# Windowed attention and two feed-forward layers: exponentials in PSUM, transposes ahead of scores, constants made on the chip

## The chip, the cores and the metric

One core of one Trainium2 chip runs the whole program in one launch. The metric is the device time of an execution in microseconds; three executions of the kernel before took 841.26, 841.40 and 842.33 us, with a median of 841.4 us. The profile is of one more execution.

## The reference

Attention over 4 batches, 8 heads, 576 positions and a head size of 64, in a causal window of 64 positions, and then two feed-forward layers over the 2304 tokens.

```python
scores = scale * np.matmul(q, k.transpose(0, 1, 3, 2))
mask = (rel >= 0) & (rel < window)             # rel = row - column, window = 64
scores = np.where(mask, scores, -1000000000.0)
scores = scores - np.max(scores, axis=-1, keepdims=True)
attn = np.exp(scores)
attn = attn / (np.sum(attn, axis=-1, keepdims=True) + 1e-09)
x = np.matmul(attn, v)                         # then (2304, 512)
x = ((x @ w1) * (x @ w2)) @ w3 @ w_out         # 512 -> 1024 -> 1024 -> 512
h = x @ w_in                                   # 512 -> 2048
out = (h * sigmoid(h)) @ w_out2
```

All of it is float32. The weights come in float64; the kernel reads their words and makes float32 of them on the chip.

## The kernel before

**Stages.** Phase W (`phase_w`, to about 93 us) multiplies w3 by w_out, in 64 float32 matmuls of 128x512 (L582), and turns the float64 words of w_out, w3, w1 and w2 into float32: an ACT pair (L125, L128), two DVE instructions (L138, L141) and a POOL add (L145) for each tile of 512 KB. Six blocks of 384 tokens follow (`phase_a`), each with 16 units of 12 matmuls (the products with w1 and w2, L618) and 8 units of 12 (the product w3 w_out, L648). The last block is merged with the second layer, which runs alone from about 410 us to the end. The order of all instructions is written out by hand; every engine runs its own in that order.

**Attention** is cut into 72 groups (128 rows, two heads). They are threaded through phase W (14 groups) and through the blocks, 12 to a block, by `half`: two halves make a group's step, and in the blocks every unit is preceded by one half, so that PE has 24 matmuls of a block between two steps. A group g passes through: scores on PE into a PSUM tile `s` that has one buffer (`scores`, L329 for the first 17 groups in plain float32, L333 and L337 after that); a masked reduction on DVE for each head, which leaves the scaled scores in the SBUF tile `sm` and their minimum in `nm` (L344, with the mask from the tile `consts`); an exponential on ACT for each head, in place in `sm`, with the sum of each row (`exps`, L355); sum, reciprocal and the multiply of the two heads on DVE (`normalise`, L363, L365, L367); three transposes on PE into the tile `t` (L377), from which ACT and DVE make the operands of the next product (`split_t`, L383 to L392); and the values' product on PE (L404 to L406, L411, L412), with its sums on ACT, DVE and POOL (L419 to L423).

The order within an even half, which stands around the change:

```python
if g < NG:
    scores(g)
squeeze(unit_of[0])
if 2 <= g <= NG + 1:
    sums.append(values(g - 2))
    ...
if 1 <= g <= NG:
    split_t(g - 1, transposes(g - 1))
if g < NG:
    exps(g)
```

The odd half normalises g, ends the sums of g - 2 and prepares the operands of g + 2. `fill` puts pieces of the weight conversions between the instructions of `scores` and `normalise` on DVE.

**The start.** POOL sets the empty corners of the tiles `kq` and `klo` (L531, L534). SP requests, one after the other, two weight tiles, q and k of group 0, masks and identity (`consts`, 192 KB), two weight tiles, q and k of group 1, another mask (128 KB), two weight tiles, and v of groups 0 to 2. The third mask follows in step 9 of phase W. In each of the 16 steps of phase W the loop first finishes the conversions that are due (`steps_to`), then runs the halves that are due (`halves_to`), then more conversions, then the matmuls.

## Time and profile before

| | |
|---|---|
| median of three executions | 841.4 us (841.26 to 842.33) |
| the profiled execution | 841.24 us, of which its instructions span 839.5 us |
| granted TensorE clock | 1.000 |
| busy: PE, DVE, ACT, POOL | 827.4, 615.3, 561.2, 529.7 us |
| DMA | 102.66 MB, mean 122 GB/s |

The profiled execution is 0.2 us under the median. Busy times are sums over stages with different limits: DVE and ACT are far from full over the span, but not within the attention's first 400 us. Matmuls are pipelined and their ends are modelled, so a stretch in which PE is busy throughout may still hold short waits; the distance between two instructions of the same kind shows them. In the rows further on, a timeline line gives the start (us from the start of the span), the duration, the engine, the line, the operation, what it writes and reads, and in brackets the idle time of the engine before it with what ended it.

### The profile page before, as it was taken

The numbers are of one execution on the slowest core, as the hardware profiler recorded it, in microseconds if no ns is written. First come the engines' busy times: TensorE is split into PE (matmuls) and PEld (weight loads), VectorE is DVE, ScalarE is ACT, GpSimd is POOL, SyncE is SP. The second block draws the span as 40 slices with busy tenths as digits, with TensorE's granted clock in tenths as the row PEclk, the third lists the DMA queues.
The fourth block names the chain that finished last, engine by engine and source line by source line (L and its number), as shares of the span: only waits on it lengthen the run. The fifth ranks groups of instructions, "written<-read, shape, count | busy, mean of one in ns | idle before, by whom it ended". The sixth has DMA issues, their size and how long they took to land.

```text
span 839.5 us, 14173 instructions
## 1 busy us (share of the span) xinstructions
PE 827.4 (99%) x4418; PEld 745.9 (89%) x4418; DVE 615.3 (73%) x1424; ACT 561.2 (67%) x1390; POOL 529.7 (63%) x588
## 2 busy tenths in 40 slices
PE   7999999999999999999999999999999999999998
PEld 3555799999999999999999988888888888988986
DVE  7889877688888888888368698998644567644544
ACT  6889778898898898898556566556543446443433
POOL 5768666677777677677565577876454456454441
PEclk9999999999999999999999999999999999999999
DMA  9998234444544544543433522301301201201002
GB/s 320 330 321 279 72 107 128 149 127 133 167 150 142 169 156 145 170 157 103 155 134 120 194 76 76 125 26 51 102 26 56 95 26 64 88 25 51 1 1 75
DMA packets 54682, 102.66 MB, mean 122 GB/s; under 512 B 5200, under 2 KB 32592, under 8 KB 54608
## 3 DMA queue, kind: packets, MB, share of 16 engines
q1 hardware_dynamic: 51008, 96.91, 35.5%
q10 hardware_dynamic: 3600, 4.85, 1.6%
q8 instruction: 35, 0.57, 0.3%
q14 instruction: 39, 0.32, 0.1%
HBM read 88.11 MB, written 13.63 MB: 121 GB/s over the span
## 4 chain that ended last, share of the span: by engine, by line
PE 69%; POOL 8%; ACT 6%; issue 4%; DVE 1%; ACTq 0%; POOLq 0%; DVEq 0%
PE o L882 24%; PE ab L618 14%; PE hy L828 12%; PE hx L828 9%; PE x L648 6%; POOL klo L303 2%; POOL vhl L321 1%; ACT sm L355 1%; PE t L377 1%; POOL xr L423 1%; ACT qkhi L297 1%; POOL p L88 1%; POOL cv_b L189 1%; PE o L411 1%; PE s L333 1%
## 5 line engine op out<-in xcount | busy, mean ns | idle before, releaser
L882 PE MATMUL o<-hl,gp 128*128 128x512 f32 x504 | 133.3, 394 | 0.0
L618 PE MATMUL ab<-xa,hl 128*128 128x384 f32 x576 | 119.0, 341 | 0.0
L828 PE MATMUL hy<-xop,j 128*128 128x384 f32 x576 | 115.9, 335 | 0.0
L618 PE MATMUL ab<-xb,hl 128*128 128x384 f32 x570 | 115.2, 334 | 0.0
L88 POOL TENSOR_TENSOR gp<-tmp,gp 128x384 fp32r<-128x384 f32 x56 | 64.1, 1145 | 77.5 <-ACT gp L85 75.9
L828 PEld LDWEIGHTS hy<-xop,j 128*128 128x128 f32 x576 | 102.6, 188 | 9.0 <-DVE tmp L722 1.0
L882 PEld LDWEIGHTS o<-hl,gp 128*128 128x128 f32 x504 | 93.1, 188 | 13.1
L618 PEld LDWEIGHTS ab<-xb,hl 128*128 128x128 f32 x570 | 100.3, 188 | 0.0
L618 PEld LDWEIGHTS ab<-xa,hl 128*128 128x128 f32 x576 | 99.1, 188 | 0.0
L844 ACT ACTIVATE tmp<-hx 128x384 f32<-128x384 f32 x48 | 23.6, 492 | 111.5 <-DVE hx L722 67.8
L722 DVE TENSOR_TENSOR tmp<-hy,tmp 128x384 f32<-128x384 f32 x96 | 53.2, 554 | 56.1 <-PE hy L828 51.5
L828 PE MATMUL hx<-xop,j 128*128 128x384 f32 x432 | 86.6, 335 | 0.0
L882 PE MATMUL o<-hl,gq 128*128 128x512 f32 x324 | 85.9, 393 | 0.0
L88 POOL TENSOR_TENSOR gq<-tmp,gq 128x384 fp32r<-128x384 f32 x36 | 39.0, 1084 | 74.3 <-ACT gq L85 74.3
L828 PEld LDWEIGHTS hx<-xop,j 128*128 128x128 f32 x432 | 76.8, 188 | 4.1
L423 POOL TENSOR_TENSOR xr<-ot 128x128 f32<-128x128 f32 x55 | 32.7, 594 | 73.7 <-DVE ot L422 65.5
L303 POOL TENSOR_TENSOR klo<-qk,qkhi 64x192 fp32r<-64x192 f32 x110 | 67.2, 611 | 7.6 <-ACT qkhi L297 2.7
L882 PEld LDWEIGHTS o<-hl,gq 128*128 128x128 f32 x324 | 60.3, 188 | 11.2
L648 PE MATMUL x<-p,wp 128*128 128x384 f32 x360 | 69.6, 339 | 0.0
L355 ACT ACTIVATE sm<-sm,nm 128x192 f32<-128x192 f32 x144 | 64.5, 450 | 3.9 <-DVE nm L344 2.5
L648 PEld LDWEIGHTS x<-p,wp 128*128 128x128 f32 x360 | 61.9, 188 | 0.0
L145 POOL TENSOR_TENSOR cv_b<-cv_b,cv_r 128x512 int32<-128x512 int32 x32 | 48.6, 1520 | 18.8 <-DVE cv_b L141 9.4
(146 smaller groups left out, 1896.7 us busy)
## 6 DMA issues: line engine op xcount, KB each, us to landing
qk<-in_qkv SPq DMA_DIRECT2D x55, 384.0 KB, 3.1
words<-in_w_out SPq DMA_DIRECT2D x24, 512.0 KB, 5.4
r<-w_in SPq DMA_DIRECT2D x22, 512.0 KB, 3.4
words<-in_w3t SPq DMA_DIRECT2D x16, 512.0 KB, 6.5
words<-in_w SPq DMA_DIRECT2D x16, 512.0 KB, 6.2
xe<-in_w_in SPq DMA_DIRECT2D x16, 512.0 KB, 4.8
v<-in_qkv SPq DMA_DIRECT2D x55, 96.0 KB, 2.7
x2d<-x2s ACTq DMA_DIRECT2D x24, 192.0 KB, 1.9
```

The lines of the kernel that those rows point to most:

```text
L88: (nc.vector if eng_lo == "dve" else nc.gpsimd).tensor_tensor(out=lo, in0=src, in1=f32(hi), op=ALU.subtract)
L145: nc.gpsimd.tensor_tensor(out=x, in0=b, in1=self.r, op=ALU.add)
L189: nc.gpsimd.tensor_tensor(out=self.b, in0=self.b, in1=self.r, op=ALU.add)
L303: nc.gpsimd.tensor_tensor(out=k_lo[g % 2][hs, h * 192 : h * 192 + 192], in0=t[hs, n], in1=f32(hi[hs, n]), op=ALU.subtract)
L355: nc.scalar.activation(out=x, in_=x, func=AF.Exp, scale=-1.0, bias=nm[:, h : h + 1], accum_out=sums_of[g % 2][:, h, 0:1])
L423: nc.gpsimd.tensor_tensor(out=xr[:, c, r : r + 128], in0=t[:, 0:128], in1=t[:, 128:256], op=ALU.add)
L618: nc.tensor.matmul(acc, lhsT=w[:, l, fs], rhs=x[k // 2][:, k % 2, r, :], start=(k == 0 and n == 0), stop=(k == 3 and n == 2),)
L648: nc.tensor.matmul(acc, lhsT=wp[f][:, l, o * 128 : (o + 1) * 128], rhs=p[f][:, r, :], start=(f == 0 and n == 0), stop=(f == 7 and n == 2),)
L722: eng.tensor_tensor(out=out, in0=a, in1=b, op=op)
L828: nc.tensor.matmul(bank[name], lhsT=w[:, l, at + kt], rhs=x[:, kt, r, :], start=(fresh and kt == 0 and n == 0), stop=(kt == 1 and n == 2), ...
L844: nc.scalar.activation(out=sg, in_=src, func=AF.Sigmoid)
L882: nc.tensor.matmul(oacc[t], lhsT=g[:, l, cols], rhs=weights["out", 2 * p + i][:, r, :], start=(p == 0 and i == 0 and n == 0), stop=(p == P ...
```

## The change

It has four parts.

1. The exponentials are written into the scores' PSUM tile `s` and not back into `sm`; the normalising multiply reads them there and writes `sm`.
2. In the even half PE runs the values of g - 2 and the transposes of g - 1 ahead of the scores of g. What ACT and DVE do keeps its order.
3. Masks and identity are no longer loaded (458,752 bytes in three DMAs), but made on the chip: by five DVE memsets and six POOL selects at the start, and by a POOL copy with two memsets for the third mask in step 0 of phase W. The corners of `kq` are set by DVE; those of `klo` by POOL behind the first group's exponentials.
4. q and k of group 2 and v of group 0 are requested right behind the first scores, v of groups 1 and 2 in steps 0 and 1; the conversions of step 1's first part come behind its halves and not ahead of them.

```diff
--- before.py
+++ after.py
@@ -40,7 +40,7 @@
 
 
 @with_exitstack
-def tile_window_attention_ffn(ctx, tc, qkv, qkp, vp, mask, w1, w2, w3t, w_out, w_in, w_out2, out):
+def tile_window_attention_ffn(ctx, tc, qkv, qkp, vp, w1, w2, w3t, w_out, w_in, w_out2, out):
 
 
 
@@ -62,6 +62,34 @@
     consts = att.tile([128, 896], F32, name="consts", tag="mask", bufs=1)
     mask_at = (384, 0, 640)
     id_sb = consts[:, 256:384]
+
+    def select(t, op, base, rows, step, fill):
+        nc.gpsimd.affine_select(
+            out=t, in_=t, compare_op=op, fill=fill, base=base, pattern=[[step, t.shape[1]]], channel_multiplier=rows
+        )
+
+    def build_first():
+        m = consts[:, 0:256]
+        nc.vector.memset(m[:, 0:64], MASKED)
+        nc.vector.memset(m[:, 64:192], 0.0)
+        nc.vector.memset(m[:, 192:256], MASKED)
+        nc.vector.memset(id_sb, 0.0)
+        select(m[:, 64:192], ALU.is_ge, 63, -1, 1, MASKED)
+        select(m[:, 64:192], ALU.is_ge, 0, 1, -1, MASKED)
+        select(id_sb, ALU.not_equal, 0, 1, -1, 1.0)
+
+    def build_band():
+        m = consts[:, 384:640]
+        nc.vector.memset(m, 0.0)
+        select(m[:, 0:192], ALU.is_ge, -1, -1, 1, MASKED)
+        select(m[:, 64:192], ALU.is_ge, 0, 1, -1, MASKED)
+        select(m[:, 192:256], ALU.is_ge, -1, -1, 1, MASKED)
+
+    def build_across():
+        nc.gpsimd.tensor_copy(out=consts[:, 640:896], in_=consts[:, 384:640])
+        nc.gpsimd.memset(consts[64:128, 640:768], MASKED)
+        nc.gpsimd.memset(consts[64:128, 832:896], MASKED)
+
     idle_in = att.tile([128, 512], F32, name="idle_in", tag="pt3", bufs=1)
     for i in range(4):
         nc.vector.memset(idle_in[:, i * 128 : i * 128 + 128], 0.37 * i - 0.73)
@@ -346,25 +374,25 @@
                 op0=ALU.add, op1=ALU.min, scale=-(D ** -0.5), scalar=3.0e38, accum_out=nm[:, h : h + 1],
             )
         fill()
-        s_st[g] = (nm, rs)
+        s_st[g] = (nm, rs, s_ps)
 
     def exps(g):
-        nm, rs = s_st[g]
+        nm, rs, e = s_st[g]
         for h in range(2):
             x = sm[g % 2][:, h, :]
             nc.scalar.activation(
-                out=x, in_=x, func=AF.Exp, scale=-1.0, bias=nm[:, h : h + 1], accum_out=sums_of[g % 2][:, h, 0:1]
+                out=e[:, h, :], in_=x, func=AF.Exp, scale=-1.0, bias=nm[:, h : h + 1], accum_out=sums_of[g % 2][:, h, 0:1]
             )
 
     def normalise(g):
-        _, rs = s_st.pop(g)
+        _, rs, e = s_st.pop(g)
         x = sm[g % 2]
         fill()
         nc.vector.tensor_reduce(out=rs, in_=sums_of[g % 2], axis=mybir.AxisListType.X, op=ALU.add)
         fill()
         nc.vector.reciprocal(out=rs, in_=rs)
         fill()
-        nc.vector.tensor_tensor(out=x, in0=x, in1=rs.unsqueeze(2).to_broadcast([128, 2, 192]), op=ALU.mult)
+        nc.vector.tensor_tensor(out=x, in0=e, in1=rs.unsqueeze(2).to_broadcast([128, 2, 192]), op=ALU.mult)
 
     def transposes(g):
 
@@ -430,15 +458,16 @@
 
         g, odd = divmod(h, 2)
         if not odd:
+            if 2 <= g <= NG + 1:
+                sums.append(values(g - 2))
+            t_ps = transposes(g - 1) if 1 <= g <= NG else None
             if g < NG:
                 scores(g)
             squeeze(unit_of[0])
-            if 2 <= g <= NG + 1:
-                sums.append(values(g - 2))
-                if plain(g - 2):
-                    sums.pop()()
-            if 1 <= g <= NG:
-                split_t(g - 1, transposes(g - 1))
+            if sums and plain(g - 2):
+                sums.pop()()
+            if t_ps:
+                split_t(g - 1, t_ps)
             if g < NG:
                 exps(g)
         else:
@@ -528,25 +557,21 @@
 
         for t in kq:
             for h, hs in HEADS:
-                nc.gpsimd.memset(t[hs, 320 - h * 320 : 512 - h * 320], 0.0)
-        for t in k_lo:
-            for h, hs in HEADS:
-                nc.gpsimd.memset(f32(t)[hs, 192 - h * 192 : 384 - h * 192], 0.0)
+                nc.vector.memset(t[hs, 320 - h * 320 : 512 - h * 320], 0.0)
+        build_first()
+        build_band()
         spin(3)
         loads_to(2)
         load_qk(0)
-        nc.sync.dma_start(out=consts[:, 0:384], in_=mask[:, 0:384])
         loads_to(4)
         load_qk(1)
-        nc.sync.dma_start(out=consts[:, 384:640], in_=mask[:, 384:640])
         loads_to(6)
-        load_v(0)
-        load_v(1)
-        load_v(2)
         steps_to(2)
         for f in line[1].stage1():
             f()
         scores(0)
+        load_qk(2)
+        load_v(0)
         spin(1)
         line[2].stage0(0)
         exps(0)
@@ -555,21 +580,27 @@
             f()
         for x in line[1:3]:
             x.begun = True
+        for t in k_lo:
+            for h, hs in HEADS:
+                nc.gpsimd.memset(f32(t)[hs, 192 - h * 192 : 384 - h * 192], 0.0)
         done["step"] = 3
         halves[0] = 1
         acc, split_done = {}, set()
         for s in range(16):
             sw, j = divmod(s, 8)
             loads_to(ready[s + 2] + (3 if s > 5 else 1 if s > 1 else 0))
-            if s == 9:
-                nc.sync.dma_start(out=consts[:, 640:896], in_=mask[:, 640:896])
+            if s == 0:
+                build_across()
+                load_v(1)
+            if s == 1:
+                load_v(2)
             if j == 0:
                 for i in range(4):
                     acc[i] = accumulator(f"accw{sw}_{i}", [128, 512])
             for part in range(2):
                 first = ready[s + 1 if s else 0]
                 steps = first + (ready[s + 2] - first) * (part + 1) // 2
-                if s:
+                if s > 1 or s and part:
                     steps_to(steps, (nc.vector, nc.gpsimd), 3)
                 halves_to(min(W_HALVES, 2 + W_HALVES * (2 * s + part + 1) // 32))
                 steps_to(steps, (nc.vector, nc.gpsimd), 3)
...
@@ -1117,7 +1136,6 @@
         "qkv": qkv,
         "qkp": plain_scores(qkv),
         "vp": plain_values(qkv),
-        "mask": masks(),
 
         "w1": inputs["moe_w1"],
         "w2": inputs["moe_w2"],
```

How it moves instructions, at three places. On PE in the second product of block 1 (`s` are scores, `o` the values' product, `t` the transposes), before:

```order
L333 MATMUL s_2572<-qkhi_2466 128x192 x2
L337 MATMUL s_2572<-klo_80,qkhi_2466 128x384
L411 MATMUL o_2581<-pt_957,vhl_2468 128x256 x2
L412 MATMUL o_2581<-pt_955,vhl_2468 128x4x64
L377 MATMUL t_2585<-consts,sm_77 128x128 x3
```

and with the change:

```order
L439 MATMUL o_2595<-pt_980,vhl_2491 128x256 x2
L440 MATMUL o_2595<-pt_978,vhl_2491 128x4x64
L405 MATMUL t_2599<-consts,sm_77 128x128 x3
L361 MATMUL s_2603<-qkhi_2489 128x192 x2
L365 MATMUL s_2603<-klo_80,qkhi_2489 128x384
```

The same five rows in another order: the scores stand behind the transposes, which stand where the scores stood but for the values' product.

On ACT in a block, from the last instructions of `split_t` to the sums of the values' product, with the semaphores that each waits for, before:

```order
L85 CAST p_2810<-a_3_3088 128x384 [waits DVE_49]
L387 CAST pt_957<-t_3143 128x2x128 [waits PE_49,Activation_49]
L389 CAST pt_955<-t_3143 64x64 [waits Activation_49] x2
L355 ACTIVATE sm_77,es_86<-sm_77,nm_3133 128x192 [waits DVE_49,Activation_49] x2
L632 COPY a_4_3169<-ab_8_3156 128x384 [waits PE_49]
```

and with the change, one place in such a block:

```order
L113 CAST p_2833<-a_0_2872 128x384 [waits DVE_49]
L415 CAST pt_979<-t_2918 128x2x128 [waits PE_49]
L417 CAST pt_977<-t_2918 64x64 x2
L383 ACTIVATE s_2922,es_87<-sm_78,nm_2926 128x192 [waits DVE_49,PE_49,Activation_49]
L383 ACTIVATE s_2922,es_87<-sm_78,nm_2926 128x192 [waits Activation_49]
L663 COPY a_1_2954<-ab_2_2941 128x384 [waits DMAHW2_49,PE_49]
```

The exponentials write `s` in place of `sm`. The first now waits for PE and DVE, the second for ACT itself: in the built program the count that it waits for is the one that the first raises.

On DVE at the start of phase W, behind the reduction of group 1, up to its normalising multiply and the conversion pair after it, before:

```order
L138 TENSOR_SCALAR cv_z<-cv_b 128x512
L141 SCALAR_TENSOR_TENSOR cv_b<-words,cv_z 128x512
L138 TENSOR_SCALAR cv_z<-cv_b 128x512
L141 SCALAR_TENSOR_TENSOR cv_b<-words,cv_z 128x512
L138 TENSOR_SCALAR cv_z<-cv_b 128x512
L363 TENSOR_REDUCE rs_198<-es_87 128x2
L141 SCALAR_TENSOR_TENSOR cv_b<-words,cv_z 128x512
L365 RECIPROCAL rs_198<-rs_198 128x2
L367 TENSOR_TENSOR sm_78<-sm_78,rs_198 128x384
L138 TENSOR_SCALAR cv_z<-cv_b 128x512
L141 SCALAR_TENSOR_TENSOR cv_b<-words,cv_z 128x512
```

and with the change:

```order
L166 TENSOR_SCALAR cv_z<-cv_b 128x512
L169 SCALAR_TENSOR_TENSOR cv_b<-words,cv_z 128x512
L166 TENSOR_SCALAR cv_z<-cv_b 128x512
L169 SCALAR_TENSOR_TENSOR cv_b<-words,cv_z 128x512
L391 TENSOR_REDUCE rs_225<-es_87 128x2
L393 RECIPROCAL rs_225<-rs_225 128x2
L395 TENSOR_TENSOR sm_78<-s_222,rs_225 128x384
L166 TENSOR_SCALAR cv_z<-cv_b 128x512
L169 SCALAR_TENSOR_TENSOR cv_b<-words,cv_z 128x512
```

The sum, the reciprocal and the multiply of group 1 (L363, L365, L367, now L391, L393, L395) stood behind three pairs of conversions and stand behind two.

## Rows read from the trace of the kernel before

**Rows 1.** Windows: length; busy us of PE, PEld, DVE, ACT, POOL; PEclk, DMA share, GB/s.
```profile
10.00:93.00 83.00, 78.16 (x277) 42.23 (x276) 73.48 (x174) 69.97 (x169) 60.30 (x48) 1.00 0.86 287
280.00:400.00 120.00, 119.61 (x746) 118.70 (x746) 103.31 (x336) 105.09 (x310) 87.48 (x120) 1.00 0.46 144
```

**Rows 2.** Timeline, 257 to 263 us: one group's exponentials, and two transposes.
```profile
257.55 0.52 PE L377 MATMUL t<-consts,sm 128*128 128x128 f32 x3
259.62 0.52 ACT L85 CAST q<-a 128x384 fp32r<-128x384 f32 x1 [0.26 <-DVE a L634]
260.76 0.46 ACT L355 ACTIVATE sm<-sm,nm 128x192 f32<-128x192 f32 x1
261.12 0.19 ACT L355 ACTIVATION_READ_ACCUMULATOR sm<-sm,nm 128x1 f32 x1
261.22 0.44 ACT L355 ACTIVATE sm<-sm,nm 128x192 f32<-128x192 f32 x1
261.56 0.19 ACT L355 ACTIVATION_READ_ACCUMULATOR sm<-sm,nm 128x1 f32 x1
261.78 0.16 DVE L363 TENSOR_REDUCE rs<-es 128x2 f32<-128x4 f32 x1 [0.22 <-ACT sm L355]
262.88 0.52 PE L377 MATMUL t<-consts,sm 128*128 128x128 f32 x3
```

**Rows 3.** Timeline, PE: the transposes of groups 23, 35, 46 and 58.
```profile
147.19 0.49 PE L377 MATMUL t<-consts,sm 128*128 128x128 f32 x3
210.11 0.49 PE L377 MATMUL t<-consts,sm 128*128 128x128 f32 x3
268.22 0.52 PE L377 MATMUL t<-consts,sm 128*128 128x128 f32 x3
332.10 0.52 PE L377 MATMUL t<-consts,sm 128*128 128x128 f32 x3
```

**Rows 4.** By line: shortest, median and longest ns of the normalising multiply, another multiply.
```profile
L367 DVE TENSOR_TENSOR sm<-sm,rs x72: 557/558/1642, 10.7 to 399.2; 128x384 f32<-128x384 f32 x72
L634 DVE TENSOR_TENSOR a<-ab,a x48: 546/558/561, 98.5 to 445.5; 128x384 f32<-128x384 f32 x48
```

**Rows 5.** Timeline, 282 to 286 us: POOL, the normalising multiply of group 49, ACT.
```profile
282.64 1.01 POOL L88 TENSOR_TENSOR xb<-xr,xb 128x384 fp32r<-128x384 f32 x1
282.71 1.36 DVE L367 TENSOR_TENSOR sm<-sm,rs 128x384 f32<-128x384 f32 x1
285.65 0.52 ACT L85 CAST xb<-xr 128x384 fp32r<-128x384 f32 x1 [1.61 <-POOL xr L423]
```

**Rows 6.** Groups by line and form: two ACT copies of 128x384, from PSUM and SBUF.
```profile
L632 ACT COPY a<-ab 128x384 f32<-128x384 f32 x42 | 20.2, 481 | 5.6 <-PE ab L618 4.5
L85 ACT CAST p<-a 128x384 fp32r<-128x384 f32 x30 | 15.4, 514 | 19.8 <-DVE a L634 19.3
```

**Rows 7.** DMA issues of the first 30 us; timeline, 10 to 33 us, DVE and PE.
```profile
consts<-in_mask SPq DMA_DIRECT2D x1, 192.0 KB, 4.2
consts<-in_mask SPq DMA_DIRECT2D x1, 128.0 KB, 5.1
...
10.75 1.54 DVE L367 TENSOR_TENSOR sm<-sm,rs 128x384 f32<-128x384 f32 x1
31.45 0.52 PE L377 MATMUL t<-consts,sm 128*128 128x128 f32 x3 [1.46 <-DVE sm L367]
```

**Rows 8.** Timeline, POOL: the first converted weight tile.
```profile
6.70 1.27 POOL L145 TENSOR_TENSOR wo<-cv_b,cv_r 128x512 int32<-128x512 int32 x1 [3.67 <-DVE cv_b L141]
```

**Rows 9.** Timeline, 36 to 44 us: scores, reduction and transposes of groups 4 and 5.
```profile
36.95 0.81 PE L329 MATMUL s<-kq 128*128 128x384 f32 x2
38.05 0.35 DVE L344 CUSTOM_DVE_ANT_0 sm<-s,consts 128x192 f32<-128x192 f32 x1
38.21 0.50 PE L377 MATMUL t<-consts,sm 128*128 128x128 f32 x3
43.24 0.50 PE L377 MATMUL t<-consts,sm 128*128 128x128 f32 x3
```

More of the change, by code (lines that the diff above doesn't have):

```diff
@@ L1096, in plain_values @@
     return v
-def masks():
-    r = np.arange(128)[:, None]
-    c = np.arange(192)[None, :]
-    band = (c >= r + 1) & (c <= r + WIN)
-    first = band & (c >= 64)
-    across = band & ((r < 64) | (c >= 128))
-    m = np.where(np.stack([band, first, across], 1), 0.0, MASKED)
-    m = np.concatenate([m, m[:, :, 0:64]], 2)
-    return np.concatenate([m[:, 1], np.eye(128), m[:, 0], m[:, 2]], 1).astype(np.float32)
 def kernel(**inputs):
```

## The prediction

> **What bounds the kernel now.** The windows view comes first [rows 1]. From 280 to 400 us, in the middle of the blocks, PE is busy 119.61 of 120 us, at the full clock. DVE (103.31) and ACT (105.09) have room on average, DMA (0.46) plenty. From 10 to 93 us, in phase W, PE is idle for 83.00 - 78.16 = 4.84 us, and DMA is at 0.86. So PE's work is the bound, and the change leaves that work as it is: the same matmuls and transposes in another order. It can gain or lose only where PE waits or would come to wait.
>
> Short waits hide inside busy PE. The transposes show them, since PE does the same between those of successive groups of a block [rows 3]. From group 23 to 35 it takes 210.11 - 147.19 = 62.92 us, 5.24 a group. From group 46 to 58 it takes 332.10 - 268.22 = 63.88. So a late block holds 0.96 us of stalls. The timeline of one group [rows 2] gives their source: transposes at 257.55 and 262.88, 5.33 apart, 0.09 above PE's 5.24. Between them ACT goes from one instruction to the next, with one wait: 0.26 us for the product on DVE (L634), which stands there behind the sums of ACT's own copies (L419, L420 to L421, L422). ACT's row is thus a ring: copies, DVE's sums and product, L85, the casts of the transposes, two exponentials, L632, copies again. It takes 5.33 us where PE needs 5.24, and PE is held back once the slack is gone. What matters in the blocks is each exponential's length, the gap between them, and what else delays ACT. The multiply (L367) and the reduction (L344) lie on DVE beside this ring.
>
> After about 400 us there is no attention, and I expect nothing there.
>
> **The change, part by part.** The sum is made against the profiled execution, 841.24 us, 0.2 under the median of 841.4.
>
> *The multiply reads PSUM.* It takes 0.56 us at the median and up to 1.64 [rows 4]. The long ones run beside a POOL instruction: at 282.71 one takes 1.36, beside L88 which began 0.07 earlier, and ACT later waits 1.61 for POOL's sums (L423), which stand behind it [rows 5]. L634, another 128x384 multiply with one input in PSUM, runs beside POOL as often and never exceeds 0.561 in 48 cases [rows 4]. With its input in PSUM the multiply should stay at 0.56. Three block edges with attention on both sides have such long multiplies ahead of a block that drifts; the last delays the ring by 1.36 - 0.56 = 0.80. I take -0.8 for each, bounds 0 (ACT's wait has another cause as well) and -0.96 (all stalls of the block). By the Trainium skill ("Perfetto Trace Analysis", Optimizing Scalar/DVE Operations) a DVE access costs about 60 ns in SBUF and 125 in PSUM, which speaks against this edit; the trace disagrees, 558 ns for both at the median [rows 4], and by the page the multiply, which is beside the ring, would be 0.07 longer.
>
> *The exponentials write PSUM.* Two effects. Before, the second starts at 261.22, 0.10 ahead of the end of the first's sum (261.12 + 0.19 = 261.31) [rows 2]. Now it waits for a count that the first raises. The reduction L363, which waits for the second, starts 0.03 after that one's sum has ended (261.56 + 0.19 = 261.75, then 261.78). If the first's count comes as late, the second starts at 261.31 + 0.03 = 261.34, which is +0.12 for each group. Bounds: 0, if the count is raised ahead of the sum, and +0.21, if the wait adds as much again as the overlap that it removes. Against it, each exponential may be shorter: an ACT copy from PSUM takes 481 ns, a cast from SBUF 514 [rows 6], 33 less. No row has ACT writing PSUM; if the destination acts like the source, two save 0.066. The bounds on the net are -0.07 (shorter, no wait) and +0.21; I take +0.10, between 0.12 - 0.066 = 0.06 and the plain 0.12, nearer the latter because the wait has a row and the saving has none. For a block of 12 groups this is +1.2, against the 0.8 saved: +0.4 net. Three such blocks: **+1.2**. The first block whose ring is slower than PE had slack and no stall (group 23 to 35); it loses slack both to a longer ring and to scores behind the transposes: **+0.5**, bounds 0 and the 0.96 of a late block.
>
> *Transposes ahead of scores.* Nothing on PE by itself. The scores take 0.81 us in plain float32 [rows 9] and come behind about 1 us more of PE work (values and 0.50 of transposes). In the blocks the reduction follows the scores by over 2 us, so this is hidden. In phase W it is not where DVE reduces at once: in group 5 scores start at 36.95, end at 37.76, the reduction starts at 38.05 [rows 9]. There the transposes of group 4 wait until 38.21; behind them and the values the scores now end near 39 in the old times, 38.2 when the start is 0.8 to 1 us earlier. I put +0.75 on group 5's transposes and +0.95 on the next ones of this kind, some of it repaid by idle time: **+1.7**, bounds 0 and 2.5.
>
> *The start.* The first multiply takes 1.54, so 0.98 over the median, and PE's transposes of group 3 wait 1.46 for DVE [rows 7]. Two loads of masks, 320 KB or 0.33 MB, leave a DMA stretch that moves 287 GB/s [rows 1, 7], about 1.1 us. Group 1's multiply goes ahead of one conversion pair. These overlap, and I take **-1.0** at group 3, bounds 0 and -2. Later multiplies in phase W that are long give **-0.3**. The five DVE memsets and the corners of kq lie in DVE's idle time ahead of its first conversion; the copy for the third mask goes on POOL between conversions; if these covers were gone, they would cost about 0.6 us each at most (L67 sets four 128x128 tiles in about that). The early q and k of group 2 are worth at most some tenths that PE waits for DMA.
>
> *Six selects on POOL.* The trace has none. Below, nothing; above, 1.27 us each like POOL's 128x512 addition, 7.6 in all. POOL idles 3.67 us before its first addition at 6.70 [rows 8], and loses the corners' memsets. At the low end all is hidden. At the high end the first conversion is some 2 us late. They are 128 to 192 wide, so I take them as hidden: **0**, bounds 0 and +2.
>
> Sum: 841.24 + 1.2 + 0.5 + 1.7 - 1.0 - 0.3 = 843.3 us, **slower by 1.9**.
>
> **The rivals.** 0.2% or 1.7 us is about what a measurement of this kernel can tell from no change: faster means below 839.7, slower above 843.1.
>
> *No change: the saving pays for the wait.* The net of the exponentials is 0.065, so 12 of them cost the 0.8 that the multiply saves, and the blocks give 0. Phase W's +0.4 remains, less any slack found: about 841.5. For it: the PSUM copy's 33 ns [rows 6]. Against: no row of an ACT write there. The Trainium skill ("ScalarE: Activation LUTs", Step-by-step: what each stage is for) says that ScalarE writes PSUM faster than SBUF; no run here shows it yet, and by that rule alone this rival would be the likelier.
>
> *Faster: the ring gets shorter.* If the second exponential's count comes ahead of the sum, nothing is added, the ring loses up to 0.07, and with it 0.09 - 0.07 = 0.02 a group remain above PE. The three blocks then give back their 0.8 to 0.96 each; with phase W at +0.4 and a quarter of a microsecond left in each block the time is 841.24 - 3 x 0.96 + 0.4 = 838.8, rounded 838.7. It decides from a net below 0.04 a group (12 x 0.04 = 0.48, saving over 0.3 a block). For it: nothing in the trace excludes it. Against: the gap of 0.03 behind L363's sum.
>
> *Much slower: full wait or late selects.* With a net of 0.19 a block pays 12 x 0.19 - 0.8 = 1.5, three of them 4.5, and 0.8 more than nothing in the first: 841.24 + 4.5 + 0.8 = 846.5. Selects 2 us late on top of the forecast give 845.3.
>
> *The multiply stays long.* If the PSUM input does not free it from POOL, the 0.8 a block is not saved: 843.3 + 2.4 = 845.7. L634 speaks against it [rows 4]; it is in the last rival's chance.
>
> **How the numbers follow.** Forecast (843.3, its own range 842 to 844.8) 0.42, no change 0.22, faster 0.24, much slower 0.12. A quarter of the forecast's case (0.10) and all but 0.02 of the no-change case fall within 0.2%: 0.30. Faster is 0.24; slower is the rest, 0.32 + 0.02 + 0.12 = 0.46. The range goes from 838.6, the faster rival, to 846.6, the much slower one.
>
> **What would show it.** In the profile after: the second exponential starts 0.55 to 0.60 after the first (0.46 before) [rows 2], and each takes 0.43 to 0.46. No multiply beside POOL exceeds 0.57. The transposes of groups 46 and 58 are over 64 us apart (63.88 before) [rows 3]; those of group 3 start near 30.5 (31.45 before) [rows 7], those of group 5 not before 43 (43.24) [rows 9]. POOL's first addition starts at 6.7 or earlier; later, the selects cost something. I am wrong if the second exponential starts as before, or if groups 46 to 58 come under 63.5 us.

## The result, and the profile after

The change makes the kernel slower: 850.74 us (median of four executions, 849.82 to 850.78) against 841.87 of the kernel before in the same runs, a ratio of 1.0102 with a 95% interval of 1.0086 to 1.0118. That is 8.9 us; the forecast was 1.9 and the range ended at 846.6. The profiled execution took 849.82 us, its instructions span 848.0.

Where the time went is read from the transposes, as in [rows 3]. Timeline of PE after the change, groups 3, 16, 23, 35, 46 and 58 (start, duration, engine, line, operation; in brackets the idle time before it and what ended it):

```profile
31.51 0.52 PE L405 MATMUL t<-consts,sm 128*128 128x128 f32 x3 [1.70 <-DVE sm L395]
...
116.43 0.52 PE L405 MATMUL t<-consts,sm 128*128 128x128 f32 x3 [0.81 <-DVE sm L395]
...
153.57 0.49 PE L405 MATMUL t<-consts,sm 128*128 128x128 f32 x3
...
216.90 0.49 PE L405 MATMUL t<-consts,sm 128*128 128x128 f32 x3
...
275.71 0.52 PE L405 MATMUL t<-consts,sm 128*128 128x128 f32 x3 [0.18 <-DVE sm L395]
...
339.98 0.52 PE L405 MATMUL t<-consts,sm 128*128 128x128 f32 x3 [0.18 <-DVE sm L395]
```

Before, the same six were at 31.45, 110.14, 147.19, 210.11, 268.22 and 332.10 (group 16's is from the timeline, the others stand in [rows 3, 7]). So group 3 is 0.06 late, group 16 already 6.29, group 35 6.79, group 46 7.49, group 58 7.88. Three quarters of the loss arise between 31 and 116 us, in phase W and just behind it; the blocks add about 2 us, near the 1.7 of the forecast; almost nothing comes after them.

The windows show the same. Busy time of PE, PEld, DVE, ACT and POOL, then the granted clock, DMA's share and GB/s:

```profile
10.00:93.00 83.00, 73.62 (x255) 40.20 (x254) 67.93 (x164) 67.90 (x162) 54.20 (x49) 0.98 0.88 281
280.00:400.00 120.00, 119.82 (x744) 118.00 (x743) 96.70 (x326) 107.45 (x306) 84.87 (x119) 1.00 0.49 153
```

In phase W PE was idle for 4.84 us [rows 1] and is now for 9.38, and its clock is 0.98 on average. One wait stands out, that for group 8's multiply; behind it every matmul is slow for a while (PE, groups 8 and 9):

```profile
63.72 0.87 PE L405 MATMUL t<-consts,sm 128*128 128x128 f32 x3 [2.21 <-DVE sm L395]
64.38 1.49 PE L357 MATMUL s<-kq 128*128 128x384 f32 x2
...
70.41 0.50 PE L405 MATMUL t<-consts,sm 128*128 128x128 f32 x3
```

The three transposes take 0.87 us instead of 0.52, the scores 1.49 instead of 0.81 [rows 9]. Windows of 2 us give the granted clock (the number behind POOL's):

```profile
60.00:62.00 2.00, 1.51 (x9) 0.89 (x7) 1.46 (x6) 1.02 (x5) 2.00 (x3) 1.00 0.94 220
62.00:64.00 2.00, 0.28 (x2) 0.31 (x3) 1.85 (x5) 2.00 (x5) 1.48 (x2) 0.91 0.83 245
64.00:66.00 2.00, 2.00 (x6) 1.39 (x5) 0.95 (x3) 1.32 (x4) 2.00 (x3) 0.50 0.61 236
66.00:68.00 2.00, 2.00 (x4) 0.72 (x4) 1.35 (x7) 1.32 (x5) 0.79 (x1) 0.74 0.23 58
```

PE works 0.28 us of the two between 62 and 64; then the clock is at 0.50, the lower of its two levels (1.2 GHz), until about 67. From group 8 to 9 it takes 6.69 us, 5.05 before.

Part of the wait ahead of group 8's transposes arises within the group. DVE and ACT in group 8 after the change (L372 is the reduction, of which the accumulator row is the second head's last, L383 the exponential, L391 the sum that starts the normalising):

```profile
60.22 0.35 DVE L372 CUSTOM_DVE_ANT_0 sm<-s,consts 128x192 f32<-128x192 f32 x1
...
60.77 0.08 DVE L372 DVE_READ_ACCUMULATOR2_ANT nm<- 128x1 f32 x1
60.95 0.42 ACT L383 ACTIVATE s<-sm,nm 128x192 f32<-128x192 f32 x1 [1.88 <-DVE nm L372]
61.53 0.42 ACT L383 ACTIVATE s<-sm,nm 128x192 f32<-128x192 f32 x1
62.11 0.16 DVE L391 TENSOR_REDUCE rs<-es 128x2 f32<-128x4 f32 x1 [0.65 <-ACT s L383]
```

And before, where the accumulator row is the first head's:

```profile
58.03 0.35 DVE L344 CUSTOM_DVE_ANT_0 sm<-s,consts 128x192 f32<-128x192 f32 x1
58.31 0.08 DVE L344 DVE_READ_ACCUMULATOR2_ANT nm<- 128x1 f32 x1
58.43 0.45 ACT L355 ACTIVATE sm<-sm,nm 128x192 f32<-128x192 f32 x1 [1.51 <-DVE nm L344]
58.88 0.44 ACT L355 ACTIVATE sm<-sm,nm 128x192 f32<-128x192 f32 x1
59.44 0.16 DVE L363 TENSOR_REDUCE rs<-es 128x2 f32<-128x4 f32 x1 [0.17 <-ACT sm L355]
```

From the first reduction to the sum it takes 1.89 us instead of 1.41. The second exponential starts 0.58 behind the first instead of 0.45, as the forecast had it. But the first starts 0.73 behind the reduction instead of 0.40: its target is the PSUM tile that the second head's reduction still reads, so it waits for both heads' reductions and not for its own alone. In the built program the count that it waits for is the one that the second reduction raises, and it starts 0.10 behind that one's end; before, it started 0.04 behind the first's. This wait was not in my forecast. The two waits are 0.48 us of the 1.39 by which T(7) to T(8), from the transposes of group 7 to those of group 8, has grown (7.42 us, 6.03 before); the experiments give the rest.

The multiplies and exponentials, shortest, median and longest in ns, after, and the exponential before:

```profile
L395 DVE TENSOR_TENSOR sm<-s,rs x72: 557/558/559, 10.3 to 407.6; 128x384 f32<-128x384 f32 x72
L383 ACT ACTIVATE s<-sm,nm x144: 418/425/440, 8.7 to 406.6; 128x192 f32<-128x192 f32 x144
```

```profile
L355 ACT ACTIVATE sm<-sm,nm x144: 437/454/488, 8.9 to 397.8; 128x192 f32<-128x192 f32 x144
```

No multiply is over 0.559 us (up to 1.642 before [rows 4]), and an exponential is 0.029 shorter into PSUM than into SBUF. Both are what the edit was to bring. On POOL, the six selects took 1.76 us together and were over by 4.7; its first addition starts at 6.72, as before [rows 8]:

```profile
2.94 1.76 POOL L67 TENSOR_SCALAR_AFFINE_SELECT consts<-consts 128x128 f32<-128x128 f32 x6 [2.49 <-DVE consts L74]
6.72 1.28 POOL L173 TENSOR_TENSOR wo<-cv_b,cv_r 128x512 int32<-128x512 int32 x1 [2.02 <-DVE cv_b L169]
```

### The profile page after: what moved, and what is told of

It reads as the page before. It is cut to its first block, busy times and chain, and to the rows that moved or that the text cites. A ratio compares the mean times of both kernels' runs of the same rounds, so it can differ in the third digit from the quotient of the medians.

```text
span 848.0 us, 13884 instructions
## 1 busy us (share of the span) xinstructions
PE 830.6 (98%) x4418; PEld 747.3 (88%) x4418; DVE 604.7 (71%) x1433; ACT 569.1 (67%) x1390; POOL 523.0 (62%) x593
## 4 chain that ended last, share of the span: by engine, by line
PE 64%; ACT 17%; DVE 7%; issue 4%; ACTq 0%; DMA 0%; POOL 0%; DVEq 0%; SPq 0%
PE o L913 24%; PE hy L859 12%; PE hx L859 9%; PE ab L649 9%; PE x L679 5%; ACT s L383 5%; PE accw L613 2%; DVE a L665 2%; ACT pt L417 2%; DVE ot L450 1%; ACT ot L448 1%; ACT a L663 1%; ACT ot L447 1%; ACT p L113 1%; PE t L405 1%
## 5 line engine op out<-in xcount | busy, mean ns | idle before, releaser
L649 PE MATMUL ab<-xa,hl 128*128 128x384 f32 x576 | 116.5, 336 | 0.0
L649 PEld LDWEIGHTS ab<-xa,hl 128*128 128x128 f32 x576 | 101.8, 188 | 0.8
L383 ACT ACTIVATE s<-sm,nm 128x192 f32<-128x192 f32 x144 | 61.1, 424 | 15.0 <-DVE nm L372 12.3
```

What stands on the lines that cost most here:

```text
L383: nc.scalar.activation(out=e[:, h, :], in_=x, func=AF.Exp, scale=-1.0, bias=nm[:, h : h + 1], accum_out=sums_of[g % 2][:, h, 0:1])
L649: nc.tensor.matmul(acc, lhsT=w[:, l, fs], rhs=x[k // 2][:, k % 2, r, :], start=(k == 0 and n == 0), stop=(k == 3 and n == 2),)
```

## The experiments

Each run is timed against the kernel before on the same chip, in five rounds. T(g) is the start of the transposes of group g.

### The parts by themselves

**Order alone**: the kernel before with part 2.

```diff
+            if 2 <= g <= NG + 1:
+                sums.append(values(g - 2))
+            t_ps = transposes(g - 1) if 1 <= g <= NG else None
             if g < NG:
                 scores(g)
...
```

> The kernel before with part 2 of the change alone: values and transposes ahead of scores, exponentials still written in place to SBUF. Theory A (scores behind the transposes close a loop in phase W: transposes, scores, reduction, exponentials, multiply, next transposes, with conversions queued between them on DVE and ACT): PE waits at the transposes of groups 5, 8, 11 and 16, T(16) is 3 to 6 us later than before (110.14), the blocks from group 36 to 70 take no more than before, total 844.5 to 847.5. Theory B (the cost is the second exponential's wait and the PSUM tile that is held until the multiply): 841 to 842.5, T(16) within 1 us of before. Theory C (the start: selects, early requests): as B, 841 to 842.5.

Measured: 844.23 us, ratio 1.0033 (1.0021 to 1.0046), a little under theory A's range. T(3) to T(16) takes 81.71 us (78.69 before), and in the blocks T(46) to T(58) only 63.22 (63.88 before):

```profile
271.89 0.52 PE L377 MATMUL t<-consts,sm 128*128 128x128 f32 x3
...
335.11 0.52 PE L377 MATMUL t<-consts,sm 128*128 128x128 f32 x3
```

So the order costs 3.0 us in phase W and saves 0.66 in a late block. The multiply of group 48, 1.64 us before and thus one of the longest of [rows 4], takes 0.60 here with both inputs in SBUF: it starts 0.15 ahead of POOL's long addition (L189), where it started 0.07 behind it before. Of the 0.66, 0.40 lie there, between T(47) and T(48). The block's saving that I gave to PSUM can be had from the order.

**PSUM alone**: the kernel before with part 1.

```diff
-                out=x, in_=x, func=AF.Exp, scale=-1.0, ...
+                out=e[:, h, :], in_=x, func=AF.Exp, scale=-1.0, ...
...
-        nc.vector.tensor_tensor(out=x, in0=x, in1=rs...
+        nc.vector.tensor_tensor(out=x, in0=e, in1=rs...
```

> The kernel before with part 1 alone: exponentials in the scores' PSUM tile, scores still ahead of values and transposes. The one score tile is now free only after the multiply, so the scores of g wait for the multiply of g - 1 and so do values and transposes behind them. Theory A (the loop through scores is the cost, whichever edit closes it): as slow as the whole change or slower, 847 to 853, T(16) 5 to 9 us late, and two more tenths of a us a group in the late blocks. Theory B (the second exponential's wait, 0.10 to 0.13 a group where ACT's ring bounds): T(16) within 1 us of before, 843 to 844.5. Theory C: 841 to 844.

Measured: 855.54 us, 1.0162 (1.0146 to 1.0177), T(16) 8.82 late. That is over the range of theory A, whose loop it fits: with scores first, they wait for the multiply that frees their tile (4.17 us ahead of group 2's scores, the longest), and the values and transposes behind them wait too. With the new order the same edit costs less, as the next run shows.

**PSUM and order**, parts 1 and 2 without 3 and 4 (both edits above).

> Parts 1 and 2 together without the masks made on the chip and the early requests. Theory A: nearly all of the loss, 848 to 852, the late blocks as in the whole change (groups 46 to 58 in 64.3 us). Theory B: 843 to 845. Theory C (the loss of phase W belongs to parts 3 and 4): 843 to 845.

Measured: 851.66 us, 1.0119 (1.0103 to 1.0135); T(46) to T(58) 64.20. The loss of the whole change is here.

**Start alone**, parts 3 and 4, and **masks alone**, part 3 (their edits are in the diff ahead).

> Parts 3 and 4 alone: masks and identity made on the chip, early requests, step 1's conversions behind its halves; exponentials and order as before. Theory A: T(1) 0.5 to 1.6 us earlier than before (19.74), gone or halved by T(3), total 840 to 842. Theory B: as A. Theory C: T(16) 3 us or more late, total 845 to 848.

> Masks and identity made on the chip without the early requests and without the move of step 1's conversions. Theory A: the 0.33 MB of loads saved at the start are worth some tenths at T(1) and T(2) and nothing from T(3) on, total 841 to 842; the gain of 0.8 of parts 3 and 4 then belongs to the requests. Rival: 840.5 to 841, the gain belongs to the masks.

Measured: 840.81 us, 0.9990 (0.9981 to 0.9999), and 840.98, 0.9991 (0.9982 to 0.9999). Both medians are 0.8 under the kernel before, at the edge of what can be told, and the masks have it without the requests, against what I expected. The profiled executions do not have it at the start: with the start alone T(1) is 0.75 early, but T(3) is 0.21 late and T(35) 0.17. They have it between groups 35 and 46: T(46) is 0.25 early there, and with the masks alone T(35) is 0.29 late and T(46) 0.05 early. Why stays open.

### Where the order pays

**Order in the blocks**: parts 3 and 4, part 2 from group 18 on, no PSUM. **Both in the blocks**: the same with part 1 from group 18 on.

```diff
+            late = g > 17
+            if late and 2 <= g <= NG + 1:
+                sums.append(values(g - 2))
+            t_ps = transposes(g - 1) if late and 1 <= g <= NG else None
             if g < NG:
                 scores(g)
...
```

> Parts 3 and 4 as in the change, part 2 only from group 18 on (the blocks), exponentials in SBUF throughout. Theory A (scores behind the transposes cost in phase W alone, where the loop is closed, and help in the blocks): T(16) at 110.3 as with the start alone, groups 46 to 58 in 63.2 us as with the order alone (63.88 before), total 838.8 to 840.0, below both kernels. Theory D (the order alone gained in the blocks only because it entered them late): groups 46 to 58 in 63.8, total 840.5 to 841.3.

> Parts 3 and 4 as in the change, parts 1 and 2 only from group 18 on. Theory A: phase W as with the start alone, T(16) at 110.3, the blocks as in the whole change (groups 46 to 58 in 64.3), total 842 to 843.5, so some 7 to 8 us of the whole change's loss belong to phase W. Theory B (the second exponential's wait is the loss wherever it runs): 847 or more.

Measured: 840.22 us, 0.9985 (0.9976 to 0.9994), and 842.93, 1.0017 (1.0008 to 1.0026), the first between its two theories, the second as theory A had it. T(46) to T(58) takes 63.29 and 64.21. Order in the blocks has the lowest median of this study, 1.4 us ahead of the kernel before, of which the start alone has 0.8; PSUM in the blocks costs 2.7 us on top of it. With phase W left as it was, 1.3 of the whole change's loss of 8.9 us remain.

**PSUM at the block edges**: order in the blocks, with part 1 for the groups whose multiply was long.

```diff
+                out=e[:, h, :] if g > 17 and g % 12 in (11, 0, 1) else x, in_=x, ...
```

> As the run with parts 3 and 4 and the order in the blocks, with the exponentials in PSUM for the three groups at each block edge alone (35 to 37, 47 to 49, 59 to 61, 71, and 23 to 25), where the multiply takes 1.2 to 1.6 us beside POOL. Theory A (a long multiply delays ACT's ring only at the edges, the wait costs 0.10 a group only where the ring has no slack): no multiply over 0.6 in the blocks' edges, groups 46 to 58 in 63.0 to 63.3, total 839.0 to 840.3. Rival (the long multiplies cost nothing once the transposes come first): 840.2 to 840.8.

Measured: 840.87 us, 0.9989 (0.9980 to 0.9998); no multiply of the edges is over 0.56, yet T(46) to T(58) is 63.63, 0.34 more than without, as the rival had it. The long multiplies that the order leaves cost less than the waits of three groups.

### The clock

**Whole, filled**: the whole change, with six dummy matmuls on PE ahead of the transposes of group 8; **whole, filled with three**.

```diff
+        for _ in range(6 if g == 8 else 0):
+            nc.tensor.matmul(t_ps, lhsT=idle_in[:, 0:128], rhs=idle_in[:, 0:384], start=True, stop=True)
         for i, at in enumerate((0, 256, 128)):
```

> The whole change with six more matmuls of 384 columns on PE, which read a constant tile and write the transposes' PSUM tile ahead of the transposes of group 8, where PE sat idle for 2.2 us and the granted clock fell to 0.79 behind it; they are about as long as that wait. Theory A (the wait itself lowers the clock, which then costs 1.6 us more): T(8) to T(9) 5.0 to 5.3 us and not 6.69, the clock 1.00 throughout, total 848.5 to 849.7. Rival (the clock falls for another reason): 850 to 851 and the clock under 1.00 again.

> As the filled run, but with three matmuls in place of six, 2.05 us by the 4.09 that six took, a little less than the wait ahead of the transposes of group 8. Theory A (the idle time lowers the clock): T(7) to T(8) 7.4 as in the whole change, T(8) to T(9) 5.0 to 5.1 and not 6.69, total 847.3 to 848.6. Rival (the clock is lowered by something else): T(8) to T(9) over 6, total 849.5 or more.

Measured: 849.23 us, 1.0095 (1.0081 to 1.0109), and 848.00, 1.0083 (1.0069 to 1.0097). Six were too many: they took 4.09 us and held PE up for longer than the wait. Three fit (the profile has two records for each), and the clock stays up:

```profile
60.76 2.15 PE L405 MATMUL t<-idle_in 128*128 128x384 f32 x6
63.05 0.55 PE L407 MATMUL t<-consts,sm 128*128 128x128 f32 x3
...
68.13 0.50 PE L407 MATMUL t<-consts,sm 128*128 128x128 f32 x3
```

T(8) to T(9) is 5.08 us and not 6.69, T(3) to T(16) 83.25 and not 84.92: with the idle time filled the clock did not fall, and that is worth 1.67 us between these two profiled executions. But idle time of this length does not always lower it. PSUM and order has the same wait ahead of the same transposes:

```profile
64.89 0.52 PE L377 MATMUL t<-consts,sm 128*128 128x128 f32 x3 [2.22 <-DVE sm L367]
```

There the clock stays at 1.00 and T(8) to T(9) is 5.05. It falls behind the wait of 1.98 us ahead of group 11 instead (T(11) to T(12) 6.75, 5.36 before), and the whole change's 1.97 us at that place leave no mark. Two of the five executions with three matmuls show a mean clock of 0.998 too, so it falls elsewhere in those; they take 849.65 and 850.00 us, the others 847.59 to 848.00.

### The waits within a group

**Second head in SBUF**: the whole change, with the second exponential in place in SBUF and one multiply per head.

```diff
-                out=e[:, h, :], in_=x, func=AF.Exp, ...
+                out=x if h else e[:, h, :], in_=x, func=AF.Exp, ...
...
+        for h in range(2):
+            nc.vector.tensor_scalar(out=x[:, h, :], in0=x[:, h, :] if h else e[:, h, :], scalar1=rs[:, h : h + 1], scalar2=None, op0=ALU.mult)
```

> The whole change, but the second head's exponential goes back in place to SBUF and so no longer waits for the first, whose result stays in PSUM; the multiply is one per head with a scalar for each row. Theory A (the wait costs 0.10 a group on ACT's ring and about as much in each turn of the loop in phase W): groups 46 to 58 in 63.1 to 63.4 us and not 64.27, T(16) 2 to 4 us late and not 6.3, total 844 to 847. Rival (it is not the wait but the hold of the PSUM tile): groups 46 to 58 at 64.2, total 849.5 to 851.

Measured: 855.52 us, 1.0166 (1.0152 to 1.0180), T(46) to T(58) 64.17. The blocks come out where the rival put them, the total where neither did. It is inconclusive, since the edit brought a cost of its own; the run with the first head in SBUF, further on, settles it. The two multiplies, from PSUM and from SBUF:

```profile
L396 DVE TENSOR_SCALAR sm<-s,rs x72: 417/418/421, 10.4 to 411.9; 128x192 f32<-128x192 f32 x72
L396 DVE TENSOR_SCALAR sm<-sm,rs x72: 309/312/1235, 10.7 to 412.2; 128x192 f32<-128x192 f32 x72
```

From SBUF it is 0.31 us alone and up to 1.24 beside POOL.

**Order, waiting**: the order alone, with the second exponential made to wait in SBUF (it overwrites one column of the first).

```diff
+            y = sm[g % 2].rearrange("p h n -> p (h n)")[:, 191:383] if h else x
-                out=x, in_=x, func=AF.Exp, ...
+                out=y, in_=x, func=AF.Exp, ...
```

> As the run with the order alone, but the second head's exponential writes its row one column to the left, over the last column of the first head's, so that it has to wait for the first; all stays in SBUF (the second head's probabilities are shifted by a column). Theory A (the wait costs about 0.10 a group on ACT's ring, wherever the result goes): groups 46 to 58 in 64.2 to 64.8 us and not 63.22, T(16) 0.5 to 2 us later than with the order alone (113.76), total 847.5 to 850 against 844.2. Rival (a write to PSUM is what costs): 844 to 845.

Measured: 858.33 us, 1.0196 (1.0182 to 1.0210), T(46) to T(58) 67.29, far more than theory A or the rival gave. ACT in a late group:

```profile
314.20 0.46 ACT L356 ACTIVATE sm<-sm,nm 128x192 f32<-128x192 f32 x1
...
314.78 0.46 ACT L356 ACTIVATE sm<-sm,nm 128x192 f32<-128x192 f32 x1
```

The second exponential starts 0.58 behind the first, as it does in PSUM in group 8, so the wait comes wherever the result goes. What it costs this run does not show: in the blocks every third group now takes 5.8 to 6.5 us, with multiplies of up to 1.64 us beside POOL.

**First head in SBUF**: the whole change, with the first exponential in place and the second in PSUM, so that neither extra wait is left. The first head's multiply writes a sum that nobody reads.

```diff
-                out=e[:, h, :], in_=x, func=AF.Exp, ...
+                out=e[:, h, :] if h else x, in_=x, func=AF.Exp, ...
...
+        for h in range(2):
+            nc.vector.tensor_scalar(
+                out=x[:, h, :], in0=e[:, h, :] if h else x[:, h, :], scalar1=rs[:, h : h + 1], scalar2=0.0,
+                op0=ALU.mult, op1=ALU.add, accum_out=None if h else nm[:, 0:1],
+            )
```

> The whole change, but the first head's exponential goes back in place to SBUF, so that it waits for its own head's reduction alone and the second, still in PSUM, waits for neither it nor more than its own reduction; the multiply is one per head, that of the first head with an accumulated sum that nobody reads. Theory A (in phase W the change's other 1.5 us are the two waits inside a group, 0.48 us a turn; in the blocks 0.10 a group): reduction's start to L391 in group 8 1.35 to 1.55 us and not 1.89, the clock falls less or not, T(3) to T(16) 82 to 83.5 us as with the order alone (81.7) and not 84.9, groups 46 to 58 under 63.6, total 843 to 846, less if the multiply stays short beside POOL. Rival (the multiply per head collides with POOL as in the run with the second head in SBUF): multiplies over 1 us, total 850 or more.

Measured: 842.24 us, 1.0009 (1.0000 to 1.0017), 0.2 us behind the kernel before, where the whole change is 8.9 behind: more is gone than expected. T(46) to T(58) is 63.56. Group 8 in this run:

```profile
59.12 0.35 DVE L372 CUSTOM_DVE_ANT_0 sm<-s,consts 128x192 f32<-128x192 f32 x1
...
59.52 0.46 ACT L383 ACTIVATE sm<-sm,nm 128x192 f32<-128x192 f32 x1 [1.74 <-DVE nm L372]
...
59.97 0.40 ACT L383 ACTIVATE s<-sm,nm 128x192 f32<-128x192 f32 x1
...
60.53 0.16 DVE L391 TENSOR_REDUCE rs<-es 128x2 f32<-128x4 f32 x1 [0.17 <-ACT s L383]
```

Reduction to sum is 1.41 us again, as before the change. The second exponential still writes PSUM and starts 0.45 behind the first, so the write adds no delay of its own; and the tile is still held until the multiply, so the rival of the second-head run falls too. T(3) to T(16) is 79.97, and neither form of the multiply is ever long:

```profile
L396 DVE TENSOR_SCALAR_CACHE_REDUCE sm<-sm,rs x72: 411/413/416, 10.2 to 399.4; 128x192 f32<-128x192 f32 x72
...
L396 DVE TENSOR_SCALAR sm<-s,rs x72: 412/418/420, 10.5 to 399.8; 128x192 f32<-128x192 f32 x72
```

**First head in SBUF, in the blocks**: the edit just above from group 18 on, with parts 3 and 4 and the order in the blocks.

> Parts 3 and 4 as in the change; from group 18 on the order of part 2 and the exponentials as in the run with the first head in SBUF; before that scores first and all in SBUF. Theory A (with neither wait in the blocks nor a multiply that collides there, PE is the bound): groups 46 to 58 in 62.9 to 63.2 us (63.29 with the order in the blocks alone), total 839.3 to 840.2. Rival (two multiplies in place of one delay the transposes): 840.2 to 841.5.

Measured: 840.57 us, 0.9984 (0.9975 to 0.9993); T(46) to T(58) 63.59, 0.30 more than with the order alone in the blocks. That is what the rival said of two multiplies in place of one, but the two kernels cannot be told apart by their times.

### What follows

From T(3) to T(16) the profiled executions take 78.69 us before, 79.97 with the first head in SBUF, 83.25 for the whole change with the clock held up, and 84.92 for the whole change. So of 6.23 us lost in phase W 1.67 belong to the clock, and 3.28 go when the first head's exponential returns to SBUF: the two waits and what they set off. The 1.28 that are left are a balance, the order less what short multiplies save; with the order alone, whose multiplies are as long as before (1.35 us for group 11), the loss is 3.02. The split is an estimate, since the kernel with the first head in SBUF also has two multiplies a group in place of one. The waits are 0.48 us in group 8; the rest of the 3.28 is other groups and knock-on. One piece of it can be seen: a conversion on DVE with two inputs in SBUF (L185) ahead of group 11's multiply takes 1.80 us in the whole change, 0.71 with the first head in SBUF. In this order:

```profile
80.39 1.80 DVE L185 TENSOR_TENSOR hl<-cv_b,hl 128x512 fp32r<-128x512 f32 x1 [0.53 <-ACT hl L181]
```

```profile
76.57 0.71 DVE L185 TENSOR_TENSOR hl<-cv_b,hl 128x512 fp32r<-128x512 f32 x1 [0.19 <-ACT hl L181]
```

## Why the prediction was wrong

**The sign was right, and so was the net of the blocks, by luck in part.** The ring of a late block is 5.43 us where it was 5.33, the +0.10 that I took, and T(46) to T(58) is 64.27, +0.39 where I had +0.4. But the saving was half of what I took, and the cost two thirds. The transposes of group 48 after the change, then its multiply and transposes before:

```profile
286.41 0.49 PE L405 MATMUL t<-consts,sm 128*128 128x128 f32 x3
```

```profile
277.51 1.64 DVE L367 TENSOR_TENSOR sm<-sm,rs 128x384 f32<-128x384 f32 x1
...
279.30 0.52 PE L377 MATMUL t<-consts,sm 128*128 128x128 f32 x3 [0.22 <-ACT xb L85]
```

From T(46) to T(48) the change saves 0.38 us, not 0.8. The kernel before loses that at group 48, whose multiply of 1.64 us ends 0.15 ahead of the transposes that read its result (the profile names a cast on ACT as the releaser, L85, which they do not read). Behind it come group 49's, whose multiply I priced on ACT's ring; they follow 5.27 later, next to nothing late. From T(48) to T(58) it costs 0.77, not 1.2, since only the last five of these distances are at the ring's 5.43 and the others are near PE's 5.24.

The two parts of the 0.10 differ from mine as well. ACT in a late group after the change:

```profile
310.15 0.42 ACT L417 CAST pt<-t 64x64 fp32r<-64x64 f32 x2
310.48 0.42 ACT L383 ACTIVATE s<-sm,nm 128x192 f32<-128x192 f32 x1
310.91 0.20 ACT L383 ACTIVATION_READ_ACCUMULATOR s<-sm,nm 128x1 f32 x1
311.15 0.43 ACT L383 ACTIVATE s<-sm,nm 128x192 f32<-128x192 f32 x1
...
311.72 0.48 ACT L663 COPY a<-ab 128x384 f32<-128x384 f32 x1
```

And before:

```profile
308.18 0.44 ACT L389 CAST pt<-t 64x64 fp32r<-64x64 f32 x2
308.64 0.46 ACT L355 ACTIVATE sm<-sm,nm 128x192 f32<-128x192 f32 x1
...
309.09 0.44 ACT L355 ACTIVATE sm<-sm,nm 128x192 f32<-128x192 f32 x1
...
309.65 0.48 ACT L632 COPY a<-ab 128x384 f32<-128x384 f32 x1
```

The second exponential comes 0.04 behind the end of the first's sum (310.91 + 0.20), as I had it (0.03). But it starts 0.67 behind the first (0.45 before), nearly twice the delay that I had; the first starts 0.33 behind the start of the casts instead of 0.46, which gives 0.13 back. From casts to copy it is 1.57 instead of 1.47. From T(16) to T(70) the loss is 8.27 - 6.29 = 1.98 where the forecast had 1.7.

**The 0.8 a block for the multiply was put in the wrong place.** The multiply did stay at 0.56. But the order alone shortens group 48's too (T(47) to T(48) is 5.24 there and in the whole change, 5.64 before), and PSUM at the edges gains nothing on top of it.

**The step that failed is "Transposes ahead of scores", with "The start" set against it.** I had +1.7 (bounds 0 and 2.5), -1.0 and -0.3 for phase W, +0.4 in all; it is +6.3. Three things went wrong; their figures are from different runs and do not add up to the 6.3. First, the order itself: 3.0 us from T(3) to T(16) alone, over my upper bound. Groups 5 and 8 lose 0.58 and 0.72 there, where I had 0.75 and 0.95; groups 11 and 16 lose 0.71 and 0.99, which I did not count. My reading is that in phase W the scores close a loop (transposes, scores, reduction, exponentials, conversions queued on DVE and ACT, multiply, next transposes), so that later scores hold up the next transposes wherever this loop has no slack; it fits these four groups, and no run opens the loop by itself. Second, I priced the wait between the exponentials on ACT's ring in the blocks and left it out of phase W, and missed the first exponential's wait altogether: 3.3 us with what they set off. Third, the clock: 1.7 us in the profiled execution. My worst case added late selects and a longer ring; none of this was in it. Its 846.5 also leaves out the +0.4 of phase W that the other rivals have, and the faster rival's sum is 838.8, not 838.7; neither slip matters here.

**The start brought little at group 3, where I had -1.0.** T(0) and T(1) are 1.01 and 1.63 early, group 0's multiply takes 0.56, but T(3) is at 31.51, not 30.5; DVE's reduction of group 2 starts at 20.84 (20.89 before). Executions scatter here: the two filled kernels do the same up to group 8 and have T(3) at 30.85 and 30.92, 0.6 and 0.5 early. With the old order it is not early at all, 31.66 with the start alone and 31.75 with the masks alone. The latter makes its requests as before, so it is not the early ones that fill the time of the loads that are gone; what does stays open.

**Rules and rows.** ScalarE does write PSUM faster than SBUF (0.425 and 0.454 us), as the Trainium skill says ("ScalarE: Activation LUTs", Step-by-step: what each stage is for); the rival that it made the likelier fell all the same, because of the waits and not of the write. The dearer DVE access to PSUM of the Trainium skill's other page ("Perfetto Trace Analysis", Optimizing Scalar/DVE Operations) does not show in the multiply (558 ns for both). The multiply per head takes 418 ns from PSUM and 312 from SBUF, but from SBUF it takes 413 as well when it also accumulates, so this difference need not be the access.

## What to carry to other kernels

When results move into a tile that another engine still reads, ask of each write which readers of the whole tile it now waits for, not only which part it overwrites; two waits of 0.1 to 0.3 us inside a group cost about 3.3 us in phase W with what they set off, and 0.10 us a group in the blocks, only in those groups that ACT's ring paces. Price a moved step in each stage apart: the same order that saves 0.66 us in a late block costs 3.0 in phase W. Look for the multiply that an engine really waits for: here the long one that held up the transposes was the one before the one priced. And where PE is made to wait, look in the granted clock for what it may lose behind the wait.

## What the runs showed of the hardware

Idle for 2.21 us, PE came back at half its clock for about 3.3 us in the profiled execution of the whole change, which cost it half of that, and with 2.15 us of dummy matmuls in the gap it stayed at full speed. Idle for 2.22 us at the same place, in PSUM and order, it stayed at full speed without them. A wait on PE can thus cost nearly twice its length, and need not.

A multiply on DVE with one scalar a row takes 0.31 us from SBUF and up to 1.24 beside POOL; in the form that also accumulates a sum it takes 0.41 and never more than 0.416 in 72 cases. The Trainium skill says both ("SBUF — State Buffer", Who interferes with whom): that instruction can take the port that DVE shares with POOL, but not in the form that writes out its accumulator; these runs agree. It is a way out of such collisions without moving data to PSUM, at 0.10 us more for each multiply.
